# Crossbar transposes, a tiled read-out and four output accumulators in a fused attention and MLP kernel

## The chip, the cores and the metric

The kernel runs on one core of a Trainium2 chip. The time is the device time of one execution in microseconds (us). The trace's span leaves out about 2 us of it. Engines are written as in the profile: PE (TensorE matmul), PEld (its weight loads), DVE (VectorE), ACT (ScalarE), POOL (GpSimd), SP (SyncE, whose DMA queue issues most stores). Tiles go by the names in the code: hp is a first product, op a second product, pt the scores, p_ps the products that form P, sr the read-out and srT its transpose. A bank is a part of PSUM, the memory for PE's results; this kernel shares out eight of them. Lower is better.

A ratio below is the mean time of one kernel's fast runs over the mean of the kernel before's fast runs of the same rounds. It is therefore not quite the ratio of the medians that stand beside it. Some runs are of a slower state, with a lower granted clock; the medians contain them, the ratios do not.

## The reference, cut to what matters

```python
B, H, S, Ns, D = (8, 8, 512, 32, 64)          # x: (B,H,S,D), state: (B,H,Ns,D)
a      = softmax(x @ state^T / sqrt(D))        # per head, 512 x 32
xread  = a @ state                             # 512 x 64
a2     = softmax(state @ x^T / sqrt(D))        # 32 x 512
sread  = a2 @ x                                # 32 x 64
attn   = concat([xread, sread], axis=2)        # heads side by side: (B*544) x 512
out    = gelu_exact(attn @ w_in) @ w_out       # w_in 512 x 2048, w_out 2048 x 512
```

## The kernel before: the parts that the change touches

`xread @ w_in` is never formed from `xread`. The kernel computes `P = state @ w_in` per head (`p_ps`), and the first product is `hp = P^T A^T`. So both x (for the scores) and a (for hp) must be transposed, and `sread` is read out through the same exponentials `e`.

```python
def xtr(b, half):                       # 16 PE transposes of x a batch, two heads at a time
    ps = ps_f.tile([128, 2, SJ, 128], BF16, name="xT_ps", tag="f")
    for ci in range(2):
        for j in range(SJ):
            nc.tensor.transpose(ps[:, ci, j, :], A.x4[:, j, 2 * half + ci, 2:130], ident)
    nc.vector.tensor_copy(out=A.xT[:, 2 * half:2 * half + 2, :, :], in_=ps)

def atr(b):                             # 8 PE transposes of a
    ...
def sread(b, t):                        # read-out: every head's e against every head's x, then a mask
    sr = ps_f.tile([128, HC, 65], FP32, name="sr", tag="f")
    for j in range(SJ):
        nc.tensor.matmul(sr, lhsT=A.e[:, 2 * j + t, :], rhs=A.x4[:, j, :, 1 + 65 * t:66 + 65 * t], ...)
    ...
def mm1(b, m):                          # first product, 2 matmuls of 512 columns, then Gelu on ACT
    ...
def mm2(u):                             # one unit: 4 of the 16 matmuls of an output tile
    j, q = r // 4, r % 4                # from batch 1 on one tile after the other, two accumulators in all
    ...
lag = 16                                # mm2(u) follows mm1 by 16 steps, a whole batch
for b in range(B):
    for s in range(MC):
        ...                             # attention of the next batch, spread over the steps
        mm1(b, s)
        done += 1
        if done > lag:
            mm2(u)
            u += 1
```

PSUM has six banks for everything (`ps_f`) and two for output accumulators (`ps_o`).

The softmax here doesn't subtract the row's maximum and nothing guards it: scores larger than these inputs give would overflow.

## Time and profile before

| | |
|---|---|
| median | 240.82 us (3 runs); 240.45 with the run measured beside the changed kernel |
| span of the profiled run | 238.6 us |
| PE busy | 223.9 us, 94% of the span |
| ACT, DVE, POOL busy | 52%, 44%, 12% |
| one batch in the steady part | 24.87 us |
| first hp, first op | 14.73 and 31.91 us |
| piece behind the last product | 3.8 us |

The page and the timeline that show this stand in the prediction. A full engine at full clock, on an almost unbroken chain of PE work, says: look for PE time to remove. Work on other engines matters only where PE waits for it. The first 32 us are where it waits.

### The profile page before, as it was taken

How to read it: one execution, taken by the hardware profiler on the slowest of the kernel's cores; microseconds unless marked ns; L12 is line 12 of the kernel's file. 1: busy time of each engine (PE TensorE's matmuls, PEld its weight loads, DVE VectorE, ACT ScalarE, POOL GpSimd, SP SyncE). 2: the span in 40 equal slices, each digit the busy share in tenths (PEclk: the TensorE clock that was granted, in tenths of full speed). 3: DMA queues.
4: the chain of work that ended last, by engine and by line, in shares of the span. 5: the costliest groups of instructions: out<-in, count | busy, mean ns of one | idle time of the engine just before them, and what ended most of it. 6: DMA issues, size and time to landing. Idle time of an engine off the chain costs nothing.

```text
span 238.6 us, 3733 instructions
## 1 busy us (share of the span) xinstructions
PE 223.9 (94%) x1535; PEld 110.6 (46%) x1564; DVE 104.8 (44%) x198; ACT 124.9 (52%) x208; POOL 28.4 (12%) x41
## 2 busy tenths in 40 slices
PE   5996797989999999999999999999999999999993
PEld 1543243535544454444545454545454444557441
DVE  3646975574646433734283428343735112111120
ACT  2577742394486447745693559454945444335100
POOL 8745003103100400030002100000000000000000
PEclk9999999999999999999999999999999999999999
DMA  7999999720822180210111111111021111121022
GB/s 192 165 191 205 202 204 127 92 88 0 105 73 88 44 135 0 79 40 16 44 47 44 44 47 44 44 48 44 0 92 44 44 44 47 52 80 44 22 69 89
DMA packets 19889, 18.36 MB, mean 77 GB/s; under 512 B 3104, under 2 KB 15648, under 8 KB 19872
## 3 DMA queue, kind: packets, MB, share of 16 engines
q0 software_dynamic: 13376, 8.09, 24.7%
q1 hardware_dynamic: 5536, 9.31, 10.5%
q10 hardware_dynamic: 960, 0.72, 1.1%
q8 instruction: 12, 0.20, 0.3%
q14 instruction: 5, 0.04, 0.1%
HBM read 17.30 MB, written 8.91 MB: 110 GB/s over the span
## 4 chain that ended last, share of the span: by engine, by line
PE 89%; DVE 5%; DMA 2%; issue 1%; ACT 1%; ACTq 0%
PE op L364 46%; PE hp L330 22%; PE p_ps L306 4%; PE sr L264 3%; PE hps L378 3%; PE ops L390 3%; PE xT_ps L192 3%; DMA x0f<-in_x_dram 2%; PE warm_ps L121 2%; PE pt L200 2%; PE aT_ps L255 1%; DVE P L320 1%; DVE x L168 1%; DVE a L231 1%; DVE sbd L148 1%
## 5 line engine op out<-in xcount | busy, mean ns | idle before, releaser
L364 PE MATMUL op<-w_out_bf,g 128*128 128x512 bf16 x498 | 128.6, 379 | 1.0
L337 ACT ACTIVATE g<-hp 128x512 bf16<-128x512 f32 x128 | 73.9, 601 | 71.5 <-PE hp L330 67.7
L364 PEld LDWEIGHTS <-g 128*128 128x128 bf16 x512 | 50.0, 98 | 58.8
L330 PE MATMUL hp<-AT,P 128*128 128x512 bf16 x243 | 73.5, 380 | 2.7 <-DVE P L320 1.5
L350 DVE COPY osb<-op 128x512 f32<-128x512 f32 x31 | 21.4, 690 | 47.5 <-PE op L364 46.9
L330 PEld LDWEIGHTS <-P 128*128 128x128 bf16 x256 | 21.6, 97 | 24.9 <-issue 7.6
L320 DVE CAST P<-p_ps 128x512 bf16<-128x512 f32 x38 | 24.3, 684 | 8.1 <-PE p_ps L306 8.1
L168 POOL COPY x<-xb 128x1024 bf16<-128x1024 bf16 x10 | 10.4, 1042 | 96.1 <-PE sr L264 57.6
L228 DVE TENSOR_REDUCE cs<-e 128x16 f32<-128x512 bf16 x16 | 10.9, 682 | 22.9 <-ACT e L210 22.9
L318 ACT CAST P<-p_ps 128x512 bf16<-128x512 f32 x26 | 14.0, 590 | 7.1 <-PE p_ps L306 6.8
L193 DVE COPY xT<-xT_ps 128x1024 bf16<-128x1024 bf16 x14 | 9.6, 688 | 7.2 <-PE xT_ps L192 7.2
L306 PE MATMUL p_ps<-w_in_bf,sbd 64*32 64x512 bf16 x256 | 11.2, 383 | 0.5
L192 PE MATMUL xT_ps<-ident,x 128*128 128x128 bf16 x112 | 8.6, 220 | 3.0 <-DVE x L168 3.0
L231 DVE TENSOR_TENSOR a<-e,ics 128x512 bf16<-128x512 bf16 x16 | 11.1, 691 | 0.6
L210 ACT ACT_TABLE_LOAD x7 | 9.0, 1283 | 3.2 <-PE pt L200 3.2
L385 ACT ACTIVATE g_sr<-hps 128x256 bf16<-128x256 f32 x16 | 6.1, 383 | 8.4 <-PE hps L378 8.0
L192 PEld LDWEIGHTS <-x 128*128 128x128 bf16 x112 | 7.3, 98 | 6.7 <-DVE x L168 3.8
L337 ACT ACT_TABLE_LOAD x8 | 10.3, 1283 | 0.1
L264 PE MATMUL sr<-x,e 128*128 128x260 bf16 x64 | 10.0, 277 | 0.0
L273 DVE RECIPROCAL inv<-sr 128x1 f32<-128x1 f32 x16 | 2.6, 165 | 16.7 <-PE sr L264 16.6
L121 PE MATMUL warm_ps<-warm 128*128 128x512 bf16 x19 | 8.1, 564 | 1.2 <-DVE warm L74 1.2
L210 ACT ACTIVATE e<-pt 128x512 bf16<-128x512 f32 x16 | 8.8, 595 | 0.8 <-PE pt L200 0.7
(50 smaller groups left out, 117.3 us busy)
## 6 DMA issues: line engine op xcount, KB each, us to landing
out_dram<-osb SPq DMA_DIRECT2D x31, 256.0 KB, 2.3
xb<-in_x_dram POOLq DMA_DIRECT2D x7, 512.0 KB, 10.5
w_in_bf<-in_moe_w_in_dram POOLq DMA_DIRECT2D x8, 256.0 KB, 9.4
w_out_bf<-in_moe_w_out_dram POOLq DMA_DIRECT2D x4, 512.0 KB, 14.4
x0f<-in_x_dram SPq DMA_DIRECT2D x2, 256.0 KB, 3.3
x0f<-in_x_dram ACTq DMA_DIRECT2D x2, 256.0 KB, 4.8
out_dram<-osb SPq DMA_DIRECT2D x8, 64.0 KB, 1.7
st_bf<-in_state_dram POOLq DMA_DIRECT2D x1, 224.0 KB, 8.9
```

Source lines behind the costliest of these rows:

```text
L121: nc.tensor.matmul(ps, lhsT=warm[:, 0:128], rhs=warm, start=True, stop=True)
L192: nc.tensor.transpose(ps[:, ci, j, :], A.x4[:, j, 2 * half + ci, 2:130], ident)
L210: nc.scalar.activation(out=A.e[:, :, 64 * half:64 * half + 64], in_=A.pt.rearrange("p j t c n -> p (j t) (c n)"), func=AF.Exp, scale=scale,)
L231: nc.vector.tensor_tensor(out=A.a[:, :, hs].rearrange("p g (c n) -> p g c n", n=NS), in0=e4, in1=ics[:, :, :].to_broadcast((128, G, 2, NS) ...
L264: nc.tensor.matmul(sr, lhsT=A.e[:, 2 * j + t, :], rhs=A.x4[:, j, :, 1 + 65 * t:66 + 65 * t], start=(j == 0), stop=(j == SJ - 1),)
L306: nc.tensor.matmul(ps[t][32 * c:32 * c + 32, :], lhsT=sbd[64 * t:64 * t + 64, b, c, 32 * t:32 * t + 32], rhs=w_in_bf[64 * t:64 * t + 64, c ...
L318: nc.scalar.copy(out=dst, in_=ps[t])
L320: nc.vector.tensor_copy(out=dst, in_=ps[t])
L330: nc.tensor.matmul(hp, lhsT=Ps[b][:, t, m * 128:(m + 1) * 128], rhs=atts[b].AT[:, t, :], start=(t == 0), stop=(t == 1),)
L337: nc.scalar.activation(out=gs[b][:, m, :], in_=hp, func=AF.Gelu)
L350: nc.vector.tensor_copy(out=osb, in_=ps)
L364: nc.tensor.matmul(ps, lhsT=gs[b][:, m, j * 128:(j + 1) * 128], rhs=w_out_bf[:, m, :], start=(m == 0), stop=(m == MC - 1),)
```

## The change

It intends to take every transpose that can be moved off PE, to shorten the read-out on PE, and to start the second product earlier.

```diff
-    ps_f = ... bufs=6 ...
-    ps_o = ... bufs=2 ...
+    ps_f = ... bufs=4 ...
+    ps_o = ... bufs=4 ...
+    def xtr_dma(b):                     # batches 2 to 7; POOL makes the dense copy x4 first
+        nc.sync.dma_start_transpose(out=A.xT..., in_=A.x4...)
+    def atr_dma(b):
+        nc.sync.dma_start_transpose(out=A.AT..., in_=A.a)
     def sread(b):
-        ... 8 matmuls 128x260, mask with hmask
+        for t in range(2):
+            for j in range(SJ):
+                for c in range(HC):
+                    nc.tensor.matmul(sr[32 * c:32 * c + 32, t, :],
+                        lhsT=A.e[:, 2 * j + t, 32 * c:32 * c + 32],
+                        rhs=A.xo[:, j, c, 1 + 65 * t:66 + 65 * t], ...)
     def srt(b):
-        ... 4 matmuls with istack
+        nc.tensor.transpose(...)
+    # start: x of batch 0 in three loads, w_out(0) early, the other loads behind norm0 of batch 0
+    M(0, 1, 2, 3); U(0, 1); pmat(0, (1,)) ...        # a unit U as soon as its quarter is through the Gelu
+    # steady: pairs M(k, k+1), then units while u < k - 4; units run over the four output tiles first
+        mm2(u // 16, u % 16 // 4, u % 4)
+    # last output tile as 384 + 128 columns in two banks
```

(Cuts are marked with dots. For batch 1 the transposes stay on PE but are done head by head; the same holds for the states.)

## The prediction

> **What bounds the kernel now.** I read the page first (engine shares, chain of waits), then the busy table by stage, then the PE timeline of one steady batch, then the timeline of the first 34 us.
>
> The page: span 238.6 us, the reported time being 240.82, so 2.2 us lie outside the span. PE is the only full engine, at full granted clock, and the chain that ended last is 89% PE:
>
> ```profile
> PE 223.9 (94%) x1535; PEld 110.6 (46%) x1564; DVE 104.8 (44%) x198; ACT 124.9 (52%) x208; POOL 28.4 (12%) x41
> ...
> PE 89%; DVE 5%; DMA 2%; issue 1%; ACT 1%; ACTq 0%
> ```
>
> DVE and ACT are half idle, so taking work from them is worth nothing by itself; taking it from PE is worth its full length. The busy table by stage (columns: stretch, its length, then busy us of PE, PEld, DVE, ACT, POOL, then clock, DMA share, GB/s) separates start, steady part and tail:
>
> ```profile
> 0.00:14.73 14.73, 11.62 (x68) 5.42 (x70) 7.34 (x17) 5.97 (x10) 11.30 (x23) 1.00 1.13 179
> 14.73:31.91 17.18, 13.70 (x124) 6.08 (x125) 13.46 (x25) 13.74 (x22) 4.14 (x5) 1.00 1.29 204
> ...
> 91.50:116.38 24.88, 24.63 (x178) 12.17 (x180) 11.82 (x22) 14.84 (x24) 2.08 (x2) 1.00 0.11 43
> ...
> 234.60:238.60 4.00, 0.21 (x1) 0.00 (x0) 0.42 (x1) 0.37 (x1) 0.00 (x0) 0.90 0.20 68
> ```
>
> One batch in the steady part takes 24.88 us and PE has hardly a gap in it. The PE timeline of that batch says what fills it (start, busy, instruction; I use differences of start times, since ends are modelled):
>
> ```profile
> 93.28 0.59 PE L330 MATMUL hp<-AT,P 128*128 128x512 bf16 x2
> 93.71 1.03 PE L364 MATMUL op<-w_out_bf,g 128*128 128x512 bf16 x4
> 94.57 0.60 PE L330 MATMUL hp<-AT,P 128*128 128x512 bf16 x2
> ...
> 96.30 1.03 PE L364 MATMUL op<-w_out_bf,g 128*128 128x512 bf16 x4
> 97.25 0.62 PE L306 MATMUL p_ps<-w_in_bf,sbd 64*32 64x512 bf16 x16
> 97.81 0.39 PE L330 MATMUL hp<-AT,P 128*128 128x512 bf16 x1
> ...
> 103.45 0.62 PE L264 MATMUL sr<-x,e 128*128 128x260 bf16 x4
> ...
> 103.91 0.59 PE L330 MATMUL hp<-AT,P 128*128 128x512 bf16 x2
> ```
>
> From 93.28 to 94.57 six products of 512 columns: 0.2155 us each. A batch has 32 of the first product (hp) and 64 of the second (op): 96 x 0.2155 = 20.69 us, a floor the change does not touch. The other 4.2 us, by the same differences: two groups of 16 p_ps products, 0.65 each (96.30 + 4 x 0.2155 = 97.16 to 97.81) = 1.31; two groups of sr, 0.46 each = 0.93; 16 transposes of x, 0.88; 8 transposes of a, 0.45; 16 score products, 0.47; the four srT products, 0.10. Sum 4.14.
>
> The start: the first hp issues at 14.73, behind the x load and the attention of batch 0. From 14.73 to 31.91 no second product runs at all, because the kernel computes the whole first batch of hp first (its lag is 16 steps). The work in that stretch is 34 hp products (7.3), five half groups of p_ps at 0.53 (2.65), and transposes, scores and sr (2.7): 12.7 of 17.18 us, so PE waits about 4.5 us there.
>
> **What the Trainium skill says.** "TensorE: Matmul & The Clock Gate", section "Wait — 56ns, not 53.3ns?", gives 215.7 ns for back-to-back warm products of 512 columns; the trace agrees with 215.5. "TensorEngine Tiling (Array Packing)", section "Key Properties": changing the tiling mode drains the array, while different tiles run in parallel. The trace agrees with both: 16 p_ps products of some 380 ns each fit in 0.65 us, yet eight-way packing alone would need only 2 x 0.2155 = 0.43, so going in and out of the mode costs about 0.2. "VectorE: DVE Perf Modes", section "The three transpose paths", has a 128x128 crossbar transpose at 1309 ns against 390 for TensorE; "DMA: Bandwidth & Descriptors", section "Latency and other measured facts", has 261 GB/s for transposes in its worse case. The kernel before has no crossbar transpose, so no run yet shows either.
>
> **The change part by part.**
>
> 1. **Transposes of x and A leave PE** for batches 2 to 7: 6 x (0.88 + 0.45) = 8.0 us, all on the path. In their place come two DMA transposes per batch, of 512 and 256 KB, and an extra dense copy of x on POOL. POOL has four copies a batch instead of two, 4 x 1.04 = 4.2 of 23 us. From the skill's 261 GB/s plus the 2.3 us that the page shows for an output DMA I estimate 4.3 and 3.3 us to landing. In a steady batch they are issued at pair 4 or 5 of 8 and first needed in the next batch, at pair 1 (x^T) or 0 (A^T): some 10 us later. Hidden, unless they take over twice my estimate. DVE also loses 1.37 + 0.69 us of copies a batch: worth nothing.
>
> 2. **Batch 1 and the state.** Batch 1 is still transposed on PE, now head by head: 32 transposes instead of 16, at 0.055 each, +0.9. The states take 28 transposes instead of 7: +1.2. Net -2.1 us of gain.
>
> 3. **Read-out (sr) on 32-column tiles.** Before, 8 products of 260 columns, of which three quarters were masked away: 0.93 us. Now 32 products of 65 columns in 8 rounds of four that can run side by side. A score product of 64 columns takes 0.47/16 = 0.029, so 8 x 0.03 = 0.24 if the four overlap fully, plus the 0.2 of mode change: about 0.5 (estimate). One transpose replaces four srT products, -0.04. Gain 0.47 x 8 batches = 3.8 us. This is the least certain term: were the four tiles not to overlap, 32 x 0.029 + 0.2 would be no gain at all.
>
> 4. **Pairs and four output accumulators.** The products are the same in number and size. In the trace going from hp to op costs nothing visible (1.29 for six), so pairs gain nothing in the steady part. What the four accumulators buy is the start: the second product of a quarter of the inner dimension can run as soon as that quarter is through the Gelu, so the lag falls from 16 steps to about 4, and the first w_out block is loaded early. PE then has second products to do while weights still arrive. Total loads do not change, and the order (w_in 0, w_out 0, w_in 1, then x 1, w_out 1, ...) follows the use. Of the 4.5 us of waiting I take 1.5 away; the first Gelus, exp table loads and evacuations still make PE wait.
>
> 5. **First hp earlier.** Three loads of x for batch 0 instead of four, heads 4 to 7 cast by DMA, weights not competing so much, scores in four steps with smaller exps, Gelu table loaded beside the transposes. The chain before is x landed 7.28, cast, transposes, copy, scores, exp, norm to 12.50, A^T 13.83, hp 14.73. With x complete near 5.5 and the same steps, hp starts near 12: -2.7 us.
>
> 6. **Tail.** Before, the last product ends at 234.8, DVE copies 0.42, ACT then 0.37, then a DMA. Now 384 columns are evacuated during the last 16 products of 128 columns, so one short copy is left: -0.5 us.
>
> 7. **Fewer buffers for everything else**: ps_f has 4 banks instead of 6, and groups of 4 p_ps tiles take all of them. The two units of second product placed behind each such group (4 x 2 x 0.2155 = 1.7 us) cover two evacuations of 0.59 or 0.69 on each engine. At the exps, table load 1.28 + two exps 1.2 + table load 1.28 hold ACT 3.8 us, while PE has 2.6 us in a pair plus two free banks. I walk through it without a stall longer than some tenths: 0.
>
> Steady batch: 20.69 + 1.31 + 0.47 + 0.5 + 0.06 = 23.0, against 24.88. Sum: 8.0 - 2.1 + 3.8 + 1.5 + 2.7 + 0.5 = 14.4, giving 240.8 - 14.4 = 226.4. Parts 3 and 4 were set carefully rather than in the middle, so I put the time at **225.5 us**.
>
> **The rivals.**
>
> *A transpose that comes late.* The DMA transposes share one queue with the output stores. x^T waits for POOL, and an A^T behind it or behind four stores could start late. Against it: the DMA engines are busy only 11% in the steady part. For it: nothing measured here. If each batch waited 1 us for it, six batches give 231 to 232; a transpose of over 12 us each would undo the gain, 236 or more. The tightest place is A^T of batch 2, issued after the four stores of batch 0 and needed right after.
>
> *PE starved by four banks instead of six.* ACT holds hp tiles 0.60 each and is blocked 3.8 us by the exps. A 0.5 us stall per batch would make 229.
>
> *The start is bound by loads.* In 14.73:31.91 the DMA engines move 204 GB/s at full share. The later loads are now held until batch 0 is normalised; if that leaves the DMA idle, the last w_out block comes late and parts 4 and 5 shrink to nothing: 229 to 230.
>
> *A better start than I take.* If most of the 4.5 us goes and hp starts at 11: 221 to 222.
>
> **Range and chances.** The 8.0 us of part 1 are nearly arithmetic; the read-out can vary by 3 us, the start by 4 either way, stalls by up to 6 upward. 225.5, range 220 to 231.5. Within 2% means above 236, which needs late transposes in every batch: faster 0.94, same 0.05, slower 0.01.
>
> **What the changed profile would show.** Right: PE gapless in a batch of 22.8 to 23.3 us; no PE transposes from batch 2 on; sr groups of 0.4 to 0.6; transposes landing in under 10 us; first hp at 11 to 13; first op within 3 us of it; the piece after the last product about 3.5. Wrong: hp or score products waiting for the DMA of AT or xT; PE waiting on Gelu or on p_ps copies each batch; sr groups near 1 us; the PE waiting for w_in or w_out after 15 us.

## The result, and the profile after

The changed kernel takes 223.06 us (median; 222.2 to 225.95, and the highest is slow), against 240.45. The ratio of fast runs is 0.9253, with a 95% interval of 0.9204 to 0.9303. The result is correct. It lies inside the predicted range and 2.4 us under the point.

First the page of the changed kernel (engine shares, then the chain by engine):

```profile
PE 209.7 (94%) x1651; PEld 101.0 (46%) x1676; DVE 81.6 (37%) x166; ACT 121.1 (55%) x215; POOL 40.5 (18%) x49
...
PE 84%; DMA 5%; DVE 5%; ACT 3%; issue 1%; SPq 0%; ACTq 0%
```

PE is still the full engine. DMA rises from 2% to 5% of the chain: a transfer now ends one of the waits, and its line is named in the list of lines, `DMA xT<-x 4%`.

Next the steady part. The score products stand once in each batch, so two of them mark one batch. From the PE timeline of the kernel before:

```profile
91.51 0.63 PE L200 MATMUL pt<-sbd,xT 128*128 128x64 bf16 x16
...
116.38 0.40 PE L200 MATMUL pt<-sbd,xT 128*128 128x64 bf16 x8
```

From that of the changed kernel, with the new read-out between:

```profile
111.79 0.63 PE L251 MATMUL pt<-sbd,xT 128*128 128x64 bf16 x16
...
125.96 0.43 PE L307 MATMUL sr<-xo,e 128*32 128x65 bf16 x32
126.32 1.04 PE L368 MATMUL hp<-AT,P 128*128 128x512 bf16 x4
...
134.82 0.63 PE L251 MATMUL pt<-sbd,xT 128*128 128x64 bf16 x16
```

One batch is 134.82 - 111.79 = 23.03 us instead of 24.87; the prediction had 23.0. No transpose of x or a stands on PE in it. The 32 read-out products hold PE from 125.96 to 126.32, 0.36 us, with about 0.1 more ahead of them, which goes with the mode change that the prediction counts.

The DMA page of the changed kernel (the last number is the median time from issue to landing):

```profile
xT<-x SPq DMA_TRANSPOSE x6, 4.6
AT<-a SPq DMA_TRANSPOSE x6, 3.5
```

The estimates were 4.3 and 3.3. The median hides one slow transfer. The view of the tile xT has the least, the median and the most:

```profile
DMA to landing us min/median/max: 4.4/4.6/8.6
```

The 8.6 belongs to the x^T of batch 3, which matters below; the other five landed in 4.4 to 5.6 us.

The start is best seen in stages. The busy table of the kernel before, same columns as in the prediction:

```profile
15.00:30.00 15.00, 11.57 (x114) 5.00 (x113) 11.70 (x21) 11.88 (x20) 4.11 (x5) 1.00 1.30 204
30.00:45.00 15.00, 13.12 (x105) 6.73 (x99) 8.92 (x20) 5.17 (x9) 2.95 (x3) 1.00 0.96 137
45.00:60.00 15.00, 13.81 (x112) 6.74 (x114) 8.90 (x19) 10.08 (x16) 2.31 (x3) 1.00 0.30 64
60.00:83.00 23.00, 22.89 (x170) 11.32 (x172) 12.06 (x23) 13.66 (x23) 3.50 (x4) 1.00 0.36 81
```

And of the changed kernel:

```profile
15.00:30.00 15.00, 14.65 (x203) 7.16 (x205) 8.05 (x18) 8.49 (x13) 2.54 (x4) 1.00 1.33 203
30.00:45.00 15.00, 13.89 (x87) 5.93 (x88) 7.21 (x15) 7.67 (x16) 9.65 (x10) 1.00 1.04 154
45.00:60.00 15.00, 13.89 (x133) 5.98 (x133) 6.12 (x12) 9.94 (x17) 5.00 (x6) 1.00 0.75 131
60.00:83.00 23.00, 20.59 (x158) 9.18 (x166) 7.54 (x15) 13.09 (x22) 4.74 (x5) 1.00 0.61 122
```

From 15 to 30 us PE is now busy 14.65 of 15 us instead of 11.57, although the loads run at the same 203 GB/s: PE has second products to do while weights arrive. But from 60 to 83 it gives 2.3 us back. The PE timeline shows one wait there:

```profile
61.58 1.89 PE L417 MATMUL op<-w_out_bf,g 128*128 128x512 bf16 x8
65.72 0.64 PE L251 MATMUL pt<-sbd,xT 128*128 128x64 bf16 x16 [2.25 <-DMA xT<-x]
```

These are the scores of batch 3, and x^T is not there. The timeline of the SP queue says why:

```profile
39.52 5.10 SPq L383 DMA_DIRECT2D out_dram<-osb  x4
55.21 1.78 SPq L296 DMA_TRANSPOSE AT<-a  x1
57.09 3.93 SPq L208 DMA_TRANSPOSE xT<-x  x1
```

POOL had the dense x of batch 3 ready at 42.25 us, and the queue was free at 44.6. But in the program A^T of batch 2 stands ahead, and it cannot be issued before batch 2 is normalised, at 55.1. The queue is in order, so x^T waits 12 us for something that it does not need. It is also slow once it is issued, with 8.6 us to landing. In steady batches the same two transposes are both ready when their turn comes.

### The profile page after: what moved, and what is told of

Its sections match the earlier page's. It is cut to its first block, busy times and chain, and to the rows that moved or that the text cites. A ratio compares the mean times of both kernels' runs of the same rounds, so it can differ in the third digit from the quotient of the medians.

```text
span 221.9 us, 3974 instructions
## 1 busy us (share of the span) xinstructions
PE 209.7 (94%) x1651; PEld 101.0 (46%) x1676; DVE 81.6 (37%) x166; ACT 121.1 (55%) x215; POOL 40.5 (18%) x49
## 2 busy tenths in 40 slices
DMA packets 38627, 22.84 MB, mean 103 GB/s; under 512 B 21840, under 2 KB 34384, under 8 KB 38608
## 4 chain that ended last, share of the span: by engine, by line
PE 84%; DMA 5%; DVE 5%; ACT 3%; issue 1%; SPq 0%; ACTq 0%
PE op L417 45%; PE hp L368 22%; DMA xT<-x 4%; PE p_ps L344 4%; PE hps L430 3%; PE ops L442 3%; ACT g L375 2%; PE opl L395 2%; DMA st_f<-in_state_dram 1%; PE pt L251 1%; PE sr L307 1%; DVE P L358 1%; DVE sbd L137 1%; DVE a L274 1%; ACT L258 1%
## 5 line engine op out<-in xcount | busy, mean ns | idle before, releaser
L417 PE MATMUL op<-w_out_bf,g 128*128 128x512 bf16 x472 | 115.3, 379 | 1.9 <-ACT g L375 0.6
L375 ACT ACTIVATE g<-hp 128x512 bf16<-128x512 f32 x128 | 67.7, 599 | 48.0 <-PE hp L368 47.9
L417 PEld LDWEIGHTS <-g 128*128 128x128 bf16 x496 | 46.9, 98 | 60.4 <-issue 6.3
L368 PE MATMUL hp<-AT,P 128*128 128x512 bf16 x256 | 64.7, 379 | 1.5 <-ACT e L258 1.0
L358 DVE CAST P<-p_ps 128x512 bf16<-128x512 f32 x33 | 21.5, 686 | 38.4 <-PE p_ps L344 38.2
L356 ACT CAST P<-p_ps 128x512 bf16<-128x512 f32 x31 | 16.9, 587 | 23.6 <-PE p_ps L344 14.5
L176 POOL COPY xo<-xb 128x1024 bf16<-128x1024 bf16 x12 | 12.3, 1054 | 53.1 <-PE sr L307 53.1
L430 PE MATMUL hps<-XSR,w_in_bf 128*128 128x256 bf16 x64 | 8.3, 273 | 0.0
L381 DVE COPY osb<-ops 128x512 f32<-128x512 f32 x2 | 1.4, 691 | 18.2 <-PE ops L442 18.2
L430 PEld LDWEIGHTS <-w_in_bf 128*128 128x128 bf16 x64 | 6.3, 98 | 2.4
L442 PE MATMUL ops<-w_out_bf,g_sr 128*128 128x512 bf16 x31 | 7.0, 379 | 0.1
```

The source lines that it names most:

```text
L176: eng.tensor_copy(out=A.xo[:, :, c0:, 2 + 64 * t:66 + 64 * t].rearrange("p j c d -> p c j d"), in_=src[:, t, c0:],)
L356: nc.scalar.copy(out=dst, in_=ps[t])
L358: nc.vector.tensor_copy(out=dst, in_=ps[t])
L368: nc.tensor.matmul(hp, lhsT=Ps[b][:, t, m * 128:(m + 1) * 128], rhs=atts[b].AT[:, :, t, :], start=(t == 0), stop=(t == 1),)
L375: nc.scalar.activation(out=gs[b][:, m, :], in_=hp, func=AF.Gelu)
L381: nc.vector.tensor_copy(out=osb, in_=ps)
```

## The experiments

There were twelve runs: eleven variants, and the changed kernel once more. The theory: the gain is PE time removed from a path without gaps (transposes 8 us, read-out 4 us), and the rest is the start and the tail. The rivals: the transposes were hidden anyway and the order of products does it; or mode changes and late transfers give the gain back. All runs were correct.

### The transposes, undone and done alone

Changed kernel, transposes back on PE:

```diff
-                rearr(nb + 1)
-                xtr_dma(nb + 1)
+                xtr(nb + 1, (0, 1))
+                xtr(nb + 1, (2, 3))
...
-                atr_dma(nb)
+                atr(nb)
```

> The changed kernel with the crossbar transposes of batches 2 to 7 put back on PE (head by head, as it does for batch 1); all else as changed. Theory (the 8 us of part 1 are PE time removed from a gapless path): in the changed kernel's trace the 32 half-width transposes of batch 1 took 0.99 us and 8 transposes of a 0.45, so 6 x 1.44 = 8.6 us come back; the 2.3 us wait for x^T of batch 3 goes away; so +6 to +7 us, near 229.5, and a steady batch of about 24.45 instead of 23.03. Rival (the transposes were hidden anyway and the gain is from the new order of products): +0 to +2 us, steady batch near 23.1.

Measured: 231.58 us, ratio 0.9612 (0.956 to 0.9664), where the changed kernel has 0.9253. That is (0.9612 - 0.9253) x 240.5 = 8.6 us back, somewhat more than expected. One batch, from its PE timeline, is 139.83 - 115.23 = 24.60 us. This is 1.57 more than 23.03, since the head-by-head form takes 1.01 us for x (127.26 to 128.27) and 0.45 for a, and some mode change.

Kernel before, only the transposes of batches 2 to 7 moved to the queue:

```diff
-        d[0].append(lambda: xtr(nb, 0))
-        d[1] = [lambda: xtr(nb, 1)]
...
-        d[9] = [lambda: atr(nb)]
+        d[6] = [lambda: atr_dma(nb)]
+        if nb + 1 < B:
+            d[9] = [lambda: begin(nb + 1), lambda: xtr_dma(nb + 1)]
```

> The kernel before with only the transposes of x and a of batches 2 to 7 moved to the DMA queue (issued about half a batch ahead, with a dense copy of x by POOL). Theory: 6 x (0.88 + 0.45) = -8.0 us, near 232.5, and about -1.8 more if the wait of PE for the rearranged x of batch 2 at 42 us goes too. Rival (the stores and transposes on one queue make PE wait): gain under 5 us, with PE idle before pt or hp for the DMA of xT or AT.

Measured: 231.87 us, ratio 0.9633 (0.9605 to 0.9661), so -8.8 us. One batch, in the PE timeline:

```profile
87.05 0.63 PE L221 MATMUL pt<-sbd,xT 128*128 128x64 bf16 x16
...
110.58 0.63 PE L221 MATMUL pt<-sbd,xT 128*128 128x64 bf16 x16
```

23.53 us against 24.87, 1.34 less, where 0.88 + 0.45 = 1.33 was predicted. It holds without any of the other parts. (6 x 1.34 is 8.0; the other 0.8 us are within the interval and in the start, where hp began at 13.67 in this run instead of 14.73.) PE waited once for x^T (1.35 us, batch 2), in place of the 1.78 that it waited there before.

### The read-out, undone and done alone

```diff
-        for t in range(2):              # changed kernel's 32 products of 65 columns
-            for j in range(SJ):
-                for c in range(HC): ...
+        for j in range(SJ):             # the old 4 products of 260 columns for each t, mask, four srT
+            nc.tensor.matmul(sr, lhsT=A.e[:, 2 * j + t, :], rhs=A.xo[:, j, :, ...], ...)
```

> The changed kernel with the old read-out: 8 products of 260 columns, mask, and four srT products, in place of 32 products of 65 columns on 32-column tiles. Theory: per batch 0.93 + 0.10 us come back for 0.46 + 0.06, so 8 x 0.51 = +4.1 us, near 227; steady batch 23.5. Rival (mode changes eat the gain): within 1 us of the changed kernel.

Measured: 226.99 us, ratio 0.9421 (0.937 to 0.9472), +4.0 us by the ratios. In its trace a batch takes 23.53 us (112.71 - 89.18), 0.50 more. The old read-out holds PE for 0.92 us in it:

```profile
126.79 1.08 PE L309 MATMUL sr<-xo,e 128*128 128x260 bf16 x8
127.71 1.02 PE L376 MATMUL hp<-AT,P 128*128 128x512 bf16 x4
```

The same edit the other way round in the kernel before:

> The kernel before with only the read-out changed to 32-column tiles (32 products of 65 columns, one transpose in place of four srT products). Theory: 8 x 0.51 = -4.1 us, near 236.5 with the before at 240.5. Rival (the rest of the path hides it, or the mode change costs as much): within 1 us of before.

Measured: 236.8 us, ratio 0.984 (0.9794 to 0.9886), so -3.9 us; a batch takes 24.37 (89.79 - 65.42), again 0.50 less. The new read-out holds PE for 0.36 us here too:

```profile
101.81 0.43 PE L264 MATMUL sr<-x,e 128*32 128x65 bf16 x32
102.17 0.60 PE L324 MATMUL hp<-AT,P 128*128 128x512 bf16 x2
```

So the four 32-column tiles do run side by side: 32 products in 0.36 us are 0.011 each, where a score product of 64 columns takes 0.029. The two parts done alone give 8.8 + 3.9 = 12.7 of the 18.0 us that the changed kernel's ratio makes, and undone in the changed kernel they cost 8.6 + 4.0 = 12.6. No run isolates the other 5 us, the start and the tail.

### Are the transposes hidden?

```diff
         nc.sync.dma_start_transpose(out=A.xT..., in_=A.x4...)
+        nc.sync.dma_start_transpose(out=xT2..., in_=A.x4...)
```

> The changed kernel with every x^T transpose issued twice (the second into a tile nobody reads). Theory (transposes are hidden in steady batches, with some 10 us of slack): batches 4 to 7 unchanged at 23.03 us; only batches 2 and 3, where x^T is already late, may lose up to 4 us. Rival (the DMA queue is nearly the bound): every batch grows by 1 us or more, total +6 or more.

Measured: 222.68 us, ratio 0.9261 (0.923 to 0.9291), the same as the changed kernel. A batch stays at 23.03 us. Twice the x^T traffic costs nothing, so in the steady part the queue and the DMA engines are far from being a bound.

### The one late transpose

```diff
-            if p == (7 if b == 1 else 4) and nb < B:
+            if p == 4 and b > 1 and nb < B:
                 atr_dma(nb)
             ...                          # begin, rearr, xtr_dma, rearr_ones, load_x
+            if p == 7 and b == 1:
+                atr_dma(nb)
```

> The changed kernel with only the order of two DMA issues swapped: x^T of batch 3 ahead of A^T of batch 2. PE's order is identical. Theory (x^T of batch 3 is late because its issue sits behind A^T of batch 2, which waits for the normalisation, on one queue in order): it is issued near 51.5 instead of 57.1 us, lands before 60, and PE's wait of 2.25 us before the scores of batch 3 is gone: -2 to -2.4 us, near 220.8. Rival 1 (the transpose is slow because of traffic, not late): the wait stays. Rival 2: A^T of batch 2 becomes the late one and PE waits at its first hp instead, gain under 1 us.

Measured: 221.25 us, ratio 0.9191 (0.9149 to 0.9233), which is 1.5 us under the changed kernel by the ratios, less than expected, with intervals that overlap. The trace is clearer: PE waits for no transpose at all, and the scores of batch 3 start at 63.05 us instead of 65.72. x^T is issued at 44.5, earlier than I wrote: I had taken a later copy on POOL for that of batch 3. As PE's instruction order is the same, an earlier issue is enough to remove the wait, and rival 2 did not happen.

Rival 1 was half right, though: x^T of batch 3 was slow as well as late. In the changed kernel it took 8.6 us to landing, and here 11.6, where the median of both is 4.6. With 4.6 us it would have landed at 57.09 + 4.6 = 61.7, before PE was ready for it at 65.72 - 2.25 = 63.47 (an estimate from these traces). So by this estimate the wait needed both, the late issue and the slow transfer. In both runs a 512 KB load of x, issued at 56.91 and 44.22, was in flight beside it. That this load slows it is likely, but no run tests it.

A second edit was put on top, one unit of second product between the two pairs behind the scores of batch 2. There PE waited 1.0 us for a PSUM bank that an exp still held. This kernel ran with the changed kernel in the same rounds:

```diff
-            if p == 3 or p == 6 and nb < B:
+            if b == 1 and p in (3, 4):
+                U(u)
+                u += 1
+            elif p == 3 or p == 6 and nb < B:
```

> The changed kernel itself again, on the same chip and in the same rounds as the next one, so that the two can be compared: 222 to 224 us, ratio near 0.925, with one wait of PE of 1 to 2.5 us for x^T of batch 3.

> The changed kernel with x^T of batch 3 issued ahead of A^T of batch 2, and one unit of second product moved in between the two pairs of first products behind the scores of batch 2, where PE waited 1.0 us for a bank that the exp still held. Theory: the two waits shrink by about 2 and 0.6 us, so 2 to 2.6 us under the changed kernel of the same rounds (ratio near 0.915). Rival (such waits only move to the next place): under 1 us.

Measured: the changed kernel again 223.25 us, ratio 0.927 (0.9232 to 0.9308); with both edits 221.37, ratio 0.9201 (0.9166 to 0.9235). That is 0.0069 x 240.3 = 1.7 us less, a little under the 2 to 2.6 expected, and the intervals overlap a little. The traces are clearer: PE's waits of 2.5 and 1.0 us are both gone, and the scores of batch 3 start at 62.07 instead of 66.12. The first edit alone, in other rounds, had 221.25 us and a ratio of 0.9191, no worse than both together. So these two are the best versions that ran; whether the second edit adds anything to the first, the times do not show.

### Pairs or singles

```diff
-            M(k, k + 1)
+            M(k)
+            if u < k - 4:
+                U(u)
+                u += 1
+            M(k + 1)
             while u < k - 4: ...
```

> The changed kernel with first and second products alternating singly instead of in pairs from batch 1 on; same products, same lag within one unit. Theory: going from one product to the other costs nothing visible (six in 1.29 us before), so within 0.5 us; steady batch 23.0 to 23.2. Rival (pairs save a switch cost): 16 more switches a batch, +0.3 us a batch or more, +2 us in all.

Measured: 224.28 us, ratio 0.9314 (0.9232 to 0.9395), an interval that holds the changed kernel's ratio. It is wide because of one run of 225.69 us at a clock of 0.992; the two fast runs at full clock took 222.63 and 222.88. A batch in its trace takes 23.04 us, one of four 23.30. The pairs by themselves buy nothing that can be seen.

### The lag, two misses

```diff
-            while u < k - 4:
+            while u < k - 16:            # and no units in the hand-written order of batch 0
```

> The changed kernel with the second products held back by 16 units instead of 4, as in the kernel before; four accumulators, pairs, loads and attention as changed. Theory of my part 4: the short lag fills PE's waits in the first 35 us; without it those waits return, +1.5 us by the prediction, up to +4 if the loads leave nothing else to do. Steady batch unchanged at 23.0. Rival (the start is bound by loads or by the attention of batch 0, so the order of products does not matter): within 0.5 us.

Measured: 236.32 us, ratio 0.9812, 13 us slower than the changed kernel: far more than either theory said. The busy table by stage of this run:

```profile
15.00:30.00 15.00, 8.34 (x173) 4.35 (x173) 8.96 (x20) 8.69 (x13) 2.04 (x3) 1.00 1.34 203
30.00:45.00 15.00, 13.93 (x80) 5.63 (x81) 3.63 (x9) 7.96 (x15) 9.60 (x10) 0.89 1.22 156
...
60.00:83.00 23.00, 19.07 (x101) 8.41 (x104) 5.85 (x10) 11.14 (x18) 2.02 (x2) 0.85 0.52 117
```

Between 15 and 30 us PE does 6.3 us less than in the changed kernel (8.34 against 14.65). It waits 4.5 us for w_in, because the loads of w_out now sit between, uselessly early. Later it waits 4.7 us for A^T of batch 2, whose issue has come to stand behind stores that are late now. And the granted clock is 0.89 from 30 to 45 us, behind the first waits, and 0.85 from 60 to 83, where the wait for A^T stands. So the run shows that lag, load order and queue order are one design; it does not give the price of the lag alone. The next run was to do that:

> The second products held back by 16 units as in e3_late_products, but with the loads issued all at once and in the order that this needs (w_in ahead of w_out, as in the kernel before), and the first crossbar transposes of A^T and x^T placed ahead of the stores. Theory (the short lag by itself is worth what PE waited in the start of the kernel before, 4 to 5 us): 225 to 226.5, with PE waiting some 4 us between its first first product and 35 us. Rival (e3 lost its 13 us only to loads in the wrong order and to the late A^T; the lag is worth nothing): 221 to 222.5.

Measured: 235.38 us, ratio 0.9814, again slow, but for a new reason that the last run isolates.

### The loads, issued at once

```diff
-    load_rest()                          # behind the normalisation of batch 0
     ...
+    load_rest()                          # right behind the first loads; only that of batch 3 stays behind the normalisation
```

> The changed kernel with all loads but that of batch 3 issued at once instead of behind the normalisation of batch 0. Theory (the order in the queue decides, the hold only keeps POOL free for its two multiplications): within 1 us. Rival (the hold protects the first loads): first product later by 1 us or more and total +1 to +2.

Measured: 235.38 us, ratio 0.9772 (0.9725 to 0.9818; its profiled run was slow, so only waits in its first 46 us are read here). My theory was wrong by 12 us. The POOL timeline of the changed kernel:

```profile
8.49 1.05 POOL L238 TENSOR_TENSOR a<-e,ics 128x512 bf16<-128x512 bf16 x1 [2.48 <-DVE ics L236]
10.55 0.62 POOL L238 TENSOR_TENSOR a<-e,ics 128x256 bf16<-128x256 bf16 x1 [1.01 <-DVE ics L236]
11.11 0.94 POOL L95 DMA_DIRECT2D xb<-in_x_dram  x1
```

And of this run:

```profile
10.15 0.74 POOL L83 DMA_DIRECT2D w_in_bf<-in_moe_w_in_dram  x1 [1.04 <-DMA w_in_bf<-in_moe_w_in_dram]
13.07 0.74 POOL L91 DMA_DIRECT2D w_out_bf<-in_moe_w_out_dram  x1 [2.18 <-DMA w_out_bf<-in_moe_w_out_dram]
15.61 0.89 POOL L95 DMA_DIRECT2D xb<-in_x_dram  x1 [1.79 <-DMA w_in_bf<-in_moe_w_in_dram]
16.51 1.62 POOL L237 TENSOR_TENSOR a<-e,ics 128x512 bf16<-128x512 bf16 x2
```

From the tenth load on, POOL waits for an earlier load to land before it issues the next, and the two multiplications that normalise batch 0 stand behind that in the same in-order queue: at 16.51 instead of 8.49. PE's timeline in this run continues:

```profile
18.19 1.04 PE L286 MATMUL aT_ps<-ident,a 128*128 128x128 bf16 x8 [7.54 <-POOL a L237]
19.31 3.73 PE L367 MATMUL hp<-AT,P 128*128 128x512 bf16 x8
22.84 0.59 PE L416 MATMUL op<-w_out_bf,g 128*128 128x512 bf16 x1
```

PE idles 7.5 us, and then its eight first products take 22.84 - 19.31 = 3.53 us, 0.44 each, where 0.216 is usual: it came back at half rate. The busy table has a granted clock of 0.50 from 18.2 to 23 us. So the hold on the loads is no matter of bandwidth. It keeps POOL's queue free for work on the path. That is not the whole of the 12 us. In the same trace PE waits a second time, 5.6 us before srT at 45.52, for DVE. Two multiplications of DVE, usually 0.69 us each, took 1.51 and 4.24 us there, while POOL's copies, which had waited for their load of x, ran beside them. (In the profiled run of the experiment before, which was a fast one, the two took 1.5 us each and PE waited 3.0.) Why they stretch is not tested. The same fault sits in that run too, where PE waited 5.5 us for POOL, so **what the short lag is worth by itself stays open**.

## Why the prediction was right

The spans of the two profiled runs differ by 238.6 - 221.9 = 16.7 us. The ratio makes 18.0, because the profiled run of the changed kernel, 223.62 us, was 1.1 to 1.4 slower than its other fast runs; that rest is in no term. Term by term:

| term | predicted | measured | from |
|---|---|---|---|
| transposes off PE, 6 batches | 8.0 | 8.0 | 6 x 1.34 (done alone) |
| batch 1 and states on PE | -2.1 | -0.6 | below |
| read-out, 8 batches | 3.8 | 4.0 | 8 x 0.50, both ways |
| waits in the start | 1.5 | 2.3 | what is left |
| first hp earlier | 2.7 | 2.2 | 14.73 to 12.49 |
| tail | 0.5 | 0.8 | 3.8 to 2.95, last products 0.04 longer |
| sum | 14.4 | 16.7 | |

**Part 1** was right in mechanism and size, and the rival of a late transpose came true in one place only, the 2.25 us of batch 3. I had named A^T of batch 2, behind the stores, as the tightest. It arrived in time, and it was itself what held x^T of batch 3 up. The prediction called the transposes hidden unless they took over twice its estimate, with some 10 us of slack. This one took just that, 8.6 us against 4.3, and had only 63.47 - 57.09 = 6.4 us.

**Part 2** was mis-sized. I charged 0.055 us for each head-by-head transpose. But such a transpose fills half the columns of the array, and two seem to run side by side: 32 of them took 0.99 us (20.02 to 21.01), 0.031 each, hardly more than the 0.88 of the 16 wide ones. The 28 transposes of the states took about 0.9 instead of 0.4. That is -0.6 in all, and it makes up 1.5 of the 2.3 us by which the sum fell short.

**Part 3**, called the least certain, held: 0.50 us a batch against 0.47 predicted.

**Part 4**: that pairs gain nothing in the steady part is shown by the singles. That the early second products fill PE's waits is seen in the busy tables; the late-products run agrees, but it upsets the order of loads and stores too. How much they are worth is not shown: the 2.3 us in the table are what is left over, after the 2.25 us given back at x^T of batch 3 are taken off. I had looked on the hold of the later loads only as a risk to the last w_out block; the last run shows that the start needs it, for POOL's queue.

**Part 5**: the first hp at 12.49 lies in the range given, but not by the step given. The prediction took x to be complete near 5.5; its last load, issued at 1.24, took 5.7 us to landing, so about 7. PE had by then transposed the first four heads, whose loads DVE took up at 3.88 and 4.66. And the start of the kernel before varies too: in the two variants of it that leave the start as it was, hp began at 13.18 and 13.67. So the 2.2 is from one run each, and 0.7 to 1.2 by those. That the number of this part came out is partly luck.

**Part 6** held, at 0.8 us against 0.5.

**Part 7**: four banks instead of six cost at most one wait of 1.0 us, in batch 1, and none in steady batches. (The kernel before, with six, has one of 1.03 us at 51.97.) The rival of a PE starved by banks did not come.

That the point was 2.4 us too high is thus mostly the transposes of part 2, charged 1.5 us too much, and for the rest the start, whose parts are not isolated. The unit of 0.2155 us is a small misreading: 1.29 / 6 is 0.215, and 32 products in a row take 6.91 us, 0.216 each. Over 96 products that is under 0.1 us.

## What to carry to other kernels

On a path without gaps, price each removed group of instructions by differences of start times in one steady period, mode changes included: these sums were exact to some hundredths of a microsecond a batch, and held when each part was done alone. When work moves to a queue that runs in order, ask for each entry what stands ahead of it and when that can go: the longest wait that the change added, and much of the 12 us that a harmless-looking move of load instructions cost, were of this kind. And before charging a half-width PE instruction, check whether its partner runs in the other half at the same time.

## What the Trainium skill lacked or had wrong

- "TensorE: Matmul & The Clock Gate", section "Back-to-back issue gap", gives about 131 ns for each product of 512 columns in a sustained stream of weight loads and products. The streams timed here, in both kernels, ran at about 216 ns (in the changed kernel 32 products in 6.91 us, from 205.79 to 212.70), which the same page calls the isolated figure.
- "VectorE: DVE Perf Modes", section "The three transpose paths", times one transpose of 128x128 (390 ns on PE, 1309 by the crossbar). In streams the numbers are others: on PE 8 wide transposes took 0.45 us, 0.056 each; by the crossbar 16 blocks landed in 4.6 us (median), 0.29 each.
- I found on no page how many microseconds the issue of a crossbar transpose of a given size holds its queue on Trainium2. ("DMA: Bandwidth & Descriptors" counts sequencer cycles of such instructions, but only where it compares trn3 with earlier generations.) Over the runs here it was 1.2 to 2.4 us for A^T (256 KB), and 1.6 to 6.3 us for x^T (512 KB), in which nothing else leaves that queue.
